# A spectral-mixing and MLP block on one core: folds, gathers and evacuations of the first stage rearranged

**Chip, cores, metric.** One core of a Trainium2 chip (trn2). The metric is the device time of one execution in microseconds; every run here was of the fast state (none was over 1.5% above the fastest of its kernel). "The profile" is one execution recorded on the chip. In its lines PE is TensorE (PEld its weight loads), DVE VectorE, ACT ScalarE, POOL GpSimd, and L241 is line 241 of that run's kernel. TensorE is called *cold* where its 256-column matmuls start 0.21 us apart and *warm* where they start 0.11 us apart; the *granted clock* is the mean TensorE clock that the profile reports, as a share of full speed. A ratio is the mean time of one kernel's runs over the mean of the kernel before's runs of the same rounds on the same chip, so it is not quite the ratio of the medians quoted beside it.

## The reference, cut to what matters

```python
def _A_ref(x, w_r, w_i):                       # x: 1 x 2048 x 512, bf16
    X = rfft2(x.astype(float32), axes=(-2, -1))
    X = X * (w_r + 1j * w_i)                   # 2048 x 257 weights
    return irfft2(X, s=(S, D)).astype(bfloat16)

h  = x + _A_ref(layernorm(x), A_w_r, A_w_i)    # first layer norm, then spectral mixing
h2 = h + mlp_squared_relu(layernorm(h))        # 512 -> 1792 -> 512
```

The transforms are done as matmuls against sine and cosine tables that the kernel computes itself. This case is about the first 26 us: first layer norm, tables, and stage 1 of the forward transform.

## The kernel before: the parts that matter

The 2048 rows lie as 16 groups g of 128. The layer norm's 1/std is not applied to the rows but *folded* into the transform table: `KFr[g] = KF * rs1[g]`. Statistics come from VectorE (13 groups) or ScalarE (groups 3, 7, 11), the root `(var + eps)^-0.5` from GpSimd.

```python
def ln1_rstd(a, b):                            # GpSimd: add, then power -0.5
    nc.gpsimd.tensor_scalar(rs1[:, a:b], mv1[:, a:b, 1], EPS, None, ALU.add)
    nc.gpsimd.tensor_tensor(rs1[:, a:b], rs1[:, a:b], mhalf[:, 0:b - a], ALU.pow)

def ln1_fold(a, b, eng=nc.vector):
    for g in range(a, b):
        eng.tensor_scalar(KFr[:, g, :], KF[:], rs1[:, g:g + 1], None, ALU.mult)

def stage1(g0, n=0, split=False):              # two groups, 8 matmuls; n filler matmuls first
    if split:                                  # two PSUM tiles, evacuated by two engines
        two = [mm_tile("p1a"), mm_tile("p1b")]
        ...
    warm(pts[0], n)
    ...                                        # 8 matmuls xs x KFr into pts
    if split:
        for t, cp in ((0, nc.scalar.copy), (1, nc.vector.tensor_copy)):
            cp(dst[:, 2 * t:2 * t + 2], ...)
        return two[0][:, 512:1024].bitcast(BF16)
    else:
        nc.scalar.copy(dst, ...)               # whole evacuation on ScalarE

def w_reversed(i):                             # indirect DMA issued by GpSimd: the "gather"
    nc.gpsimd.indirect_dma_start(out=WB[i][:, 16:23, :]..., in_=(A_w_r, A_w_i)[i]..., ...)
```

PSUM is the memory that matmuls write to; an *evacuation* copies a tile out of it, and the program keeps four tiles of this size. In the traces each engine runs its list in the order in which it is written: in e2 below, ScalarE stood idle for 2.46 us in front of a sine whose angles were late, with an evacuation that was ready behind it. `angles_g` (GpSimd) and `sin_of(GF)` (ScalarE) make the table that stage 2 needs. The products mA and mB of the spectral loop (VectorE) read the gathered rows from their second round on.

## Time and profile before

| | kernel before |
|---|---|
| time, median of 4 runs | 183.78 us (183.73 to 183.84) |
| span in the profile | 181.9 us |
| TensorE / VectorE / ScalarE / GpSimd busy | 88% / 67% / 56% / 26% |
| first matmul of stage 2 | 22.43 us |
| second mA (VectorE) starts | 29.61 us |
| first matmul of the MLP | 62.37 us |

Busy shares average over stages with different limits. The question for each stage is which wait ends last; for the first 22 us the chain of waits answers it, and the prediction shows those lines.

### The profile page before, as it was taken

The page shows a single profiled execution, that of the slowest core. Times are in us where ns is not written, and L with a number is a line of the kernel's source. Part 1 is how long each engine was busy: PE and PEld are TensorE (multiplying, and loading weights), DVE is VectorE, ACT ScalarE, POOL GpSimd, SP SyncE. Part 2 cuts the span into 40 slices and gives each one's busy share as a digit, 9 for nine tenths or more (in the row PEclk, how much of TensorE's full clock was granted, in tenths as well). Part 3 has the DMA queues.
Part 4 walks back from the last instruction along what each step waited for, and adds up shares of the span by engine and source line. Part 5 has one row for each costly group of instructions (what it writes and reads, how often), then busy time and mean ns, then how long its engine had stood idle before and what let it go on. Part 6 is the DMA issues. An engine that isn't in the chain of part 4 may idle for free.

```text
span 181.9 us, 2667 instructions
## 1 busy us (share of the span) xinstructions
PE 160.0 (88%) x946; PEld 89.0 (49%) x946; DVE 122.2 (67%) x297; ACT 101.8 (56%) x172; POOL 46.5 (26%) x83
## 2 busy tenths in 40 slices
PE   3676896989978787999999999999999989999991
PEld 1244564666534475456643545544544434556440
DVE  7986549999957277646897248697338795359311
ACT  4976879999634278037931367922357921268200
POOL 5889910000000250204402022422022422025000
PEclk9999999999999999999999999999999999999999
DMA  5999990000000000000000000001110000110010
GB/s 159 352 425 405 378 228 23 0 0 4 2 0 0 2 4 0 2 29 29 4 0 29 29 29 4 0 0 50 36 34 0 0 0 29 58 34 0 0 58 29
DMA packets 7773, 11.19 MB, mean 62 GB/s; under 512 B 2256, under 2 KB 6224, under 8 KB 7504
## 3 DMA queue, kind: packets, MB, share of 16 engines
q1 hardware_dynamic: 7600, 10.11, 16.3%
q0 software_dynamic: 160, 0.92, 1.2%
q8 instruction: 7, 0.11, 0.3%
q14 instruction: 6, 0.05, 0.1%
HBM read 8.93 MB, written 2.10 MB: 61 GB/s over the span
## 4 chain that ended last, share of the span: by engine, by line
PE 50%; DVE 29%; ACT 9%; POOL 6%; issue 4%; DVEq 0%; POOLq 0%; ACTq 0%
PE ph L570 22%; PE po L589 20%; DVE act L574 3%; PE p L473 3%; DVE mA L379 3%; DVE mB L379 3%; DVE hs L488 2%; ACT rl L573 2%; ACT Bt L241 2%; PE p L532 2%; DVE st L497 2%; DVE st L205 2%; DVE M L392 2%; DVE Z L384 2%; ACT junk L494 1%
## 5 line engine op out<-in xcount | busy, mean ns | idle before, releaser
L570 PE MATMUL ph<-UT,W 128*128 128x384 bf16 (+2 forms) x280 | 53.2, 336 | 0.7 <-ACT UT L536 0.5
L573 ACT ACTIVATE rl<-ph,b1f 128x384 bf16<-128x384 f32 (+2 forms) x70 | 41.2, 603 | 20.9 <-PE ph L570 19.5
L589 PE MATMUL po<-W,act 128*128 128x512 bf16 x224 | 50.8, 379 | 0.0
L574 DVE TENSOR_TENSOR act<-rl 128x384 bf16<-128x384 bf16 (+2 forms) x70 | 32.5, 477 | 17.2 <-ACT rl L573 16.9
L570 PEld LDWEIGHTS <-W 128*128 128x128 bf16 x280 | 27.4, 98 | 20.8 <-issue 1.4
L589 PEld LDWEIGHTS <-act 128*128 128x128 bf16 x224 | 21.6, 98 | 27.4 <-issue 3.1
L577 POOL TENSOR_TENSOR hb<-hs,b2b 128x512 f32<-128x512 bf16 x16 | 18.4, 1153 | 57.4 <-DVE act L574 55.4
L593 DVE TENSOR_TENSOR ot<-po,hb 128x512 bf16<-128x512 f32 x16 | 11.0, 689 | 18.1 <-PE po L589 18.1
L517 ACT ACTIVATE u<-hs,nm,rs 128x512 bf16<-128x512 bf16 x6 | 4.7, 808 | 25.2 <-DVE nm L514 25.2
L231 PE MATMUL p<-KFr,xs 128*128 128x256 bf16 x28 | 8.6, 334 | 4.7 <-DVE KFr L216 4.6
L488 DVE SCALAR_TENSOR_TENSOR hs<-p,xs 128x512 bf16<-128x512 f32 x16 | 10.8, 678 | 0.1
L473 PE MATMUL p<-GI,T 128*128 128x256 bf16 x64 | 9.4, 272 | 0.4 <-DVE T L415 0.4
L502 POOL TENSOR_TENSOR nm<-mv 128x1 f32<-128x1 f32 x5 | 1.5, 291 | 30.9 <-ACT junk L494 30.9
L246 PE MATMUL idle<-ones 128*128 128x512 bf16 x37 | 9.0, 379 | 0.0
L487 PE MATMUL p<-R,KI 128*128 128x512 bf16 x16 | 6.1, 381 | 3.2 <-DVE R L483 3.2
L233 PE MATMUL p<-KFr,xs 128*128 128x256 bf16 x28 | 8.6, 335 | 0.0
L246 PEld LDWEIGHTS <-ones 128*128 128x128 bf16 x45 | 4.7, 106 | 7.8 <-POOL ones L142 2.9
L205 DVE BATCH_NORM_STATS2 st<-xs 128x6 f32<-128x512 bf16 x13 | 8.3, 673 | 0.0
L360 ACT CAST AB<-p 128x1024 bf16<-128x1024 f32 x7 | 7.1, 1014 | 1.9 <-PE p L358 1.2
L417 ACT CAST T<-p 128x1024 bf16<-128x1024 f32 x7 | 7.2, 1025 | 1.8 <-PE p L410 1.8
L330 PE MATMUL p<-GF,Bt 128*128 128x256 bf16 x64 | 8.1, 273 | 0.0
L473 PEld LDWEIGHTS <-T 128*128 128x128 bf16 x64 | 6.2, 98 | 3.5 <-ACT T L414 0.9
(135 smaller groups left out, 220.5 us busy)
## 6 DMA issues: line engine op xcount, KB each, us to landing
W<-in_B_w_dram SPq DMA_DIRECT2D x2, 1792.0 KB, 19.7
out_dram<-ot SPq DMA_DIRECT2D x16, 128.0 KB, 1.8
xs<-in_A_x_dram SPq DMA_DIRECT2D x3, 512.0 KB, 5.9
WB<-in_A_w_r_dram SPq DMA_DIRECT2D x1, 1028.0 KB, 9.6
WB<-in_A_w_i_dram SPq DMA_DIRECT2D x1, 1028.0 KB, 12.2
xs<-in_A_x_dram SPq DMA_DIRECT2D x2, 256.0 KB, 3.4
b2b<-in_B_b_dram SPq DMA_DIRECT2D x1, 128.0 KB, 8.2
b1b<-in_B_b_dram SPq DMA_DIRECT2D x1, 3.5 KB, 22.8
```

Of the source, the lines that this page charges most:

```text
L205: nc.vector.bn_stats(st[:], xs[:, g, :])
L231: nc.tensor.matmul(o, lhsT=xs[:, g, P * t:P * t + P], rhs=KFr[:, g, 0:P].unsqueeze(1).to_broadcast([P, 2, P]), start=True, stop=False)
L246: nc.tensor.matmul(o, lhsT=ones[:, 0:P], rhs=ones[:], start=True, stop=True)
L379: nc.vector.tensor_tensor(m[:], X[:], w[:, pr:pr + step + 1:step, 1:Df].unsqueeze(2).to_broadcast([P, 2, 2, 256]), ALU.mult)
L473: nc.tensor.matmul(pe[:, 256 - 256 * e:512 - 256 * e], lhsT=T2[:, lt, g].rearrange("p q s -> p (q s)"), rhs=GI[:, lt, :], start=(r == 0), ...
L488: nc.vector.scalar_tensor_tensor(hs[:, g, :], py[:], WSC, xs[:, g, :], ALU.mult, ALU.add)
L570: nc.tensor.matmul(ph[:, 0:n], lhsT=W1[:, d, bass.ts(f, P)], rhs=UT[:, d, 0:n], start=(d == 0), stop=(d == ND - 1))
L573: nc.scalar.activation(rl[:, 0:n], ph[:, 0:n], ACT.Relu, bias=b1f[:, f:f + 1], scale=1.0)
L574: sq = nc.vector.tensor_tensor(act[:, f, 0:n], rl[:, 0:n], rl[:, 0:n], ALU.mult)
L577: add = nc.gpsimd.tensor_tensor(hb[:, g, :], hs[:, g, :], b2b[:], ALU.add)
L589: nc.tensor.matmul(po[:], lhsT=act[:, f, bass.ts(i, P)], rhs=W2[:, f, :], start=(f == 0), stop=(f == NF - 1))
L593: nc.vector.tensor_tensor(ot[:], po[:], hb[:, g, :], ALU.add)
```

## The change

Its intent: take work off GpSimd, which holds up the start. All folds go to VectorE; both gathers are issued behind the last root; ScalarE's three pairs of sums come first; the evacuation of (12, 13) is split between ScalarE and VectorE as that of (14, 15) was; two table copies (KI and EI) move behind the first step of stage 3.

```diff
--- before.py
+++ after.py
@@ -260,50 +260,46 @@
     def table_neg(ks):
         nc.vector.tensor_scalar(EI[:, ks[0]:ks[-1] + 1, 2, :], EI[:, ks[0]:ks[-1] + 1, 0, :], -1.0, None, ALU.mult)
 
-    ln1_sums(3)
-    ln1_sums(7)
+    for g in (3, 7, 11):
+        ln1_sums(g)
     ln1_stats(0, 1)
     ln1_rstd(0, 2)
-    w_reversed(0)
+    angles_g(0)
     ln1_stats(2, 4, 5)
     ln1_fold(0, 2)
     stage1(0, 8)
-    ln1_sums(11)
-    angles_g(0)
     ln1_rstd(2, 6)
-    w_reversed(1)
+    angles_g(1)
     ln1_stats(6, 8, 9)
     ln1_fold(2, 6)
     stage1(2)
     ln1_rstd(6, 10)
-    ln1_fold(8, 10, nc.gpsimd)
-    angles_g(1)
     stage1(4)
     ln1_stats(10, 12)
-    ln1_fold(6, 8)
+    ln1_rstd(10, 12)
+    ln1_fold(6, 10)
+    stage1(6)
+    ln1_stats(13)
+    ln1_fold(10, 12)
+    ln1_rstd(12, 14)
     sin_of(GF[:].rearrange("p t c -> p (t c)"), fiG[:])
-    stage1(6)
-    ln1_rstd(10, 12)
-    ln1_stats(13)
-    ln1_rstd(12, 14)
     stage1(8)
     ln1_stats(14, 15)
-    ln1_fold(10, 12)
     ln1_rstd(14, 16)
+    ln1_fold(12, 14)
+    stage1(10)
     nc.gpsimd.memset(ident[:], 0.0)
     nc.gpsimd.affine_select(out=ident[:], in_=ident[:], compare_op=ALU.not_equal,
                             fill=1.0, base=0, pattern=[[-1, P]], channel_multiplier=1)
-    stage1(10)
-    ln1_fold(12, 14)
-    stage1(12)
+
+    nc.vector.tensor_scalar(GF[:, :, 255:256], GF[:, :, 255:256], 0.5, None, ALU.mult)
     ln1_fold(14, 16)
+    w_reversed(0)
+    w_reversed(1)
     nc.vector.tensor_scalar(EF[:, :, 2, :], EF[:, :, 0, :], -1.0, None, ALU.mult)
-
-    nc.vector.tensor_scalar(GF[:, :, 255:256], GF[:, :, 255:256], 0.5, None, ALU.mult)
+    stage1(12, split=True)
     tr08 = stage1(14, split=True)
     transposed(tr08, (0, 8), True)
-    nc.scalar.copy(KI[:], tr08[:, 4 * P:5 * P])
-    table_i(tr08, (0, 8))
 
     nc.gpsimd.tensor_scalar(cols[:, 4:5], pF[:, 0:1], 256.0, 128.0, ALU.mult, ALU.add)
     nc.gpsimd.tensor_scalar(cols[:, 5:6], pF[:, 0:1], 256.0, 256.0, ALU.mult, ALU.add)
@@ -419,6 +415,8 @@
     stage2(0, split=True)
     stage2(1)
     stage3(0)
+    nc.scalar.copy(KI[:], tr08[:, 4 * P:5 * P])
+    table_i(tr08, (0, 8))
     stage3(1)
     stage2(2)
     tr = mm_tile("ptr", BF16)
```

## The prediction

> **What bounds the kernel now.** I read the page's engine shares first, then the chain of waits in order of time, then the timelines of ScalarE, VectorE and GpSimd over the first 27 us, and last the busy time by stretch. TensorE is busy 88% of the span, but the change touches only the first 26 us, and there the chain of waits runs elsewhere. Its columns are start, length and piece of work:
>
> ```profile
> 9.97 0.54 POOL rs L212
> 10.52 0.70 issue
> 11.22 1.12 POOL WB L145
> 12.38 0.27 POOL rs L211
> 12.72 1.05 POOL rs L212
> 13.88 1.93 POOL KFr L216 x2
> 15.90 0.94 POOL fiG L179 x2
> 16.86 1.06 ACT GF L113
> 17.92 3.68 ACT Bt L241 x4
> 21.60 0.50 ACT Bt L238
> 22.14 0.40 PE p1a L251 x4
> 22.59 1.75 PE p L330 x16
> ```
>
> The path is GpSimd from 9.65 to 16.84 us (second gather L145, inverse roots L211/L212, two folds L216, second half of the angles L179). Then ScalarE takes over until 22.09 us with the sine of those angles (GF) and five stage-1 evacuations that could not pass it in its queue. Then stage 2 (L330) starts. The ScalarE timeline shows the same handover, with the reason for each idle stretch in brackets:
>
> ```profile
> 13.31 1.01 ACT L241 CAST Bt<-p 128x1024 bf16<-128x1024 f32 x1 [0.67 <-PE p L233]
> 15.01 1.01 ACT L241 CAST Bt<-p 128x1024 bf16<-128x1024 f32 x1 [0.69 <-PE p L233]
> 16.86 1.06 ACT L113 ACTIVATE GF<-fiG 128x1024 bf16<-128x1024 int16 x1 [0.84 <-POOL fiG L179]
> 17.83 3.77 ACT L241 CAST Bt<-p 128x1024 bf16<-128x1024 f32 x4
> 21.50 0.59 ACT L238 CAST Bt<-p1a 128x512 bf16<-128x512 f32 x1
> ```
>
> From 26.4 us the bound is VectorE and from 62.4 us TensorE; the busy-time table (PE, PEld, DVE, ACT, POOL) says so:
>
> ```profile
> 26.40:52.10 25.70, 22.23 (x167) 14.79 (x164) 25.49 (x64) 21.66 (x23) 0.27 (x1) 1.00 0.03 6
> 62.40:181.90 119.50, 111.50 (x630) 58.82 (x629) 73.04 (x164) 57.43 (x110) 25.21 (x32) 1.00 0.06 18
> ```
>
> Neither has slack to absorb an earlier start, so whatever the start of stage 2 gains should reach the end nearly whole, and nothing but that start can gain. So the question is one number: when does the first L330 matmul start, which is now 22.43 us?
>
> **What the Trainium skill says.** "SBUF — State Buffer", section "Who interferes with whom": GpSimd shares a port pair with VectorE's two-port modes, and whichever starts second waits. The trace agrees in direction: two VectorE folds beside a GpSimd fold took 0.70 us (at 13.81 us), against 0.48 us alone (at 17.99 us); it is no full block, as a GpSimd fold lasts 0.97 us. "TensorE: Matmul & The Clock Gate", section "Part 1: The HAM clock gate (the “warmup” mystery)": half clock until some 3.4 us of sustained matmuls. The trace agrees: the 256-column matmuls start 0.213 us apart from 11.40 to 14.77 us (3.37 us) and 0.109 us apart from there on. "DMA: Bandwidth & Descriptors", section "Anatomy of one DMA — SWDGE (gpsimd) path", fits 2.0 us plus bytes over 436e3 per us for one DMA. A gather here is 128 x 1799 bf16 values, 460,544 bytes, so 3.1 us; the trace has 7.9 and 7.4 us to landing, beside 400 GB/s of other loads. I use the trace's.
>
> **The change part by part.**
>
> GpSimd loses, before the angles are done, both gathers (1.24 + 1.12 us busy, some 0.4 us of issue around them) and two folds (1.93 us), 4.7 us in all. Its list, followed by hand: first root done at 7.10; angles first half 7.14 to 8.08; roots 2 to 6 wait for ScalarE's sums of g = 3 (8.34) and take 0.23 + 0.09 + 1.06, so 8.39 to 9.77; second half of angles 9.81 to 10.75; roots 6 to 10 to 12.18. So the angles that came at 16.84 are there at 10.75 us, and the sine no longer waits for GpSimd.
>
> VectorE becomes the pacemaker of the folds. Rates from its timeline: three statistics 2.08 us, two 1.42, one 0.82, four folds 0.79, two 0.38. From 8.31: statistics 6, 8, 9 to 10.39; folds 2 to 6 (roots at 9.77, before they waited until 11.06) to 11.18; statistics 10, 12 to 12.60; folds 6 to 10 to 13.39; statistics 13 to 14.21; folds 10, 11 to 14.59; statistics 14, 15 to 16.01; folds 12, 13 to 16.39; the last root comes at 17.22, so folds 14, 15 at about 17.3 to 17.65, if the half-scaling of GF ahead of them is not waiting for the sine (below). The two folds moved here cost VectorE 0.4 us, where GpSimd took 1.93.
>
> TensorE: stage 1 of (2, 3) starts 0.34 us behind its first fold, at 10.73 (was 11.40). Sixteen cold matmuls at 0.213 us last until 14.14; if warmth comes 3.4 us after the start, at 14.1, and at the latest at 14.77 as before, (6, 7) ends at 15.0 to 15.3, (8, 9) at 16.1, (10, 11) at 17.0, (12, 13) at 17.9.
>
> ScalarE: three pairs of sums now come first, 6.78 to 11.17 at 1.46 us each (the third needs its rows by 9.71; the transfers of 512 KB land in 5.9 us at the median, so about 8). An evacuation costs 0.92 us back to back, the sine 0.97, a half evacuation 0.5 to 0.59. Evacuations: (0) 11.17 to 12.08; (2) waits for its matmuls, 12.69 to 13.60; (4) 14.39 to 15.30; (6) 15.4 to 16.3; sine to 17.3; (8) to 18.2; (10) to 19.1; half of (12) to 19.6; half of (14) to about 20.2. It idles perhaps 1.5 us in between, waiting for cold matmuls; this is why I do not book the whole GpSimd gain of 6.1 us.
>
> The end of stage 1: the four PSUM tiles are handed round, and two split stages need four. By the order in the built program (14, 15) takes the tiles of (8, 9) and (10, 11), so its second half starts only when evacuation (10) is done, about 19.15 to 19.3; four matmuls of 0.11 and the tail bring VectorE's half evacuation to 19.9 to 20.6. Splitting (12) moves 0.69 us to VectorE, which is free, and saves ScalarE 0.42. The transposes wait for ScalarE's last half and take 0.29 us, so stage 2 starts at 20.5 to 20.75 by this count. For the shared port I add 0.1: the angles now lie beside the folds at 7.9 and 10.4 us. I take **20.7 us** against 22.43, a gain of **1.7 us**.
>
> Moving the two copies for the inverse tables (KI and EI, 0.16 + 0.48 us) behind the X copy takes them ahead of AB, where ScalarE was idle 0.62 us waiting for L358: by the count it is free 0.07 us before AB is wanted. Value zero.
>
> The gathers now start behind the last root and the identity: 18.0 and 19.2 us. With 7.9 and 7.4 us to land they are there at 25.9 and 26.6. The products that read their rows are the second mA and mB, at 29.61 and 30.20 before, so 27.9 and 28.5 then: 1.9 us to spare. Hidden, but not by much.
>
> Sum: −1.7 us, nothing added elsewhere: 183.8 − 1.7 = **182.1 us**, 0.9%.
>
> **The rivals.** First, **ScalarE without gaps**. It has 11.17 us plus six evacuations, a sine and two halves, 7.6 us, so 18.8 if it never waits; then VectorE's last folds and half evacuation bound stage 2 at 19.7 and the gain is 2.7 us, 181.1. For it: the idle stretches hang on when TensorE gets warm. Against it: the matmuls were cold from 8.26 to 14.77 before, and the gap at 10 us is still there. Second, **the cold clock lasts longer**: if the warm decision falls a window later, up to 0.8 us of the gain goes, 182.9. Third, **the gathers become the wait**: a landing 3 us later than assumed would stop VectorE at the second mA for a microsecond, 183.1, and much later makes it slower than before. For it: they are issued while the W1 and W2 loads still run (387 GB/s from 16.6 to 22.4 us). Against it: those loads die out by about 26 us, and before there were more of them ahead. Fourth, **stage 1 not the end**: if VectorE's spectral loop were held by something else, the gain would vanish; against it stands the table above, 25.49 of 25.70 us busy.
>
> **Range and chances.** The first rival sets the low side, the second and a mild third the high side: 181.3 to 183.1 for 8 in 10. Two per cent is 3.7 us, more than even the gapless count gives: faster 0.04. Slower by 3.7 us would need a gather landing some 7 us late: 0.02. Within 2%: 0.94.
>
> **What would show it right or wrong.** Right: in the changed profile the sine of GF no longer waits for GpSimd; the first L326 matmul (stage 2's new line) starts near 20.7; the second half of stage 1 (14, 15) waits for evacuation (10); from there everything is the old trace moved by the same amount, with stretch lengths of 25.7, 10.3 and 119.5 us kept. Wrong: VectorE idle at the second mA or mB put down to a DMA; the last stage-1 evacuations beginning much before or after 18.2 us; a spectral loop longer than 25.7 us, which would say that ScalarE's AB copies came late behind KI and EI.

## The result, and the profile after

The changed kernel ran in 182.54 us at the median of four runs (182.08 to 182.77), against 183.78: a ratio of 0.9929, interval 0.991 to 0.9949. It lies inside the stated range, 0.44 us above the stated time.

The chain of waits of the changed kernel (start, length, piece):

```profile
1.63 5.12 DMA xs<-in_A_x_dram
6.77 0.69 DVE st L205
...
10.79 0.27 DVE KFr L216
11.10 0.37 PE p L231
...
16.26 1.01 ACT Bt L241
17.28 0.95 ACT GF L113
18.23 1.82 ACT Bt L241 x2
20.05 0.98 ACT Bt L238 x2
21.08 0.40 PE p1a L251 x4
21.53 1.78 PE p L326 x16
```

GpSimd is gone from the start. The path now begins with the landing of the rows at 6.75 us, runs through VectorE's statistics and folds and TensorE's matmuls of stage 1, and ends on ScalarE again. ScalarE's timeline, with what ended each idle stretch in brackets:

```profile
13.00 1.01 ACT L241 CAST Bt<-p 128x1024 bf16<-128x1024 f32 x1 [0.85 <-PE p L233]
14.71 1.01 ACT L241 CAST Bt<-p 128x1024 bf16<-128x1024 f32 x1 [0.69 <-PE p L233]
16.26 1.01 ACT L241 CAST Bt<-p 128x1024 bf16<-128x1024 f32 x1 [0.54 <-PE p L233]
17.17 1.06 ACT L113 ACTIVATE GF<-fiG 128x1024 bf16<-128x1024 int16 x1
18.13 1.92 ACT L241 CAST Bt<-p 128x1024 bf16<-128x1024 f32 x2
```

The sine (GF) waits for nothing any more, but it comes *later* than before, 17.17 instead of 16.86 us, because one more evacuation lies ahead of it and each of the first ones waits for matmuls (0.85, 0.69, 0.54 us). Behind it stand only two whole evacuations and two halves instead of four and one: that is the gain. Stage 2 starts at 21.37 us, 1.06 earlier than before. TensorE's timeline shows why the evacuations wait:

```profile
15.32 0.42 PE L231 MATMUL p<-KFr,xs 128*128 128x256 bf16 x1
15.53 0.42 PE L233 MATMUL p<-KFr,xs 128*128 128x256 bf16 x1
...
15.95 0.27 PE L233 MATMUL p<-KFr,xs 128*128 128x256 bf16 x1
16.06 0.27 PE L231 MATMUL p<-KFr,xs 128*128 128x256 bf16 x1
```

Starts lie 0.21 us apart until about 15.8 us and 0.11 us from there: the cold clock ended a microsecond later than in the kernel before (14.77). It was not cold throughout: the first matmuls of stage 1, from 8.58 us, start 0.11 us apart, and at about 9.1 us, after an idle stretch of 2.40 us and half a microsecond of matmuls, the clock falls back. In the kernel before they were cold from the first one, at 8.26 us. The filler matmuls ahead of them already differ, though no edit touches them (first line before, second line after):

```profile
2.94 3.60 PE L246 MATMUL p<-ones 128*128 128x512 bf16 x8 [2.94 <-POOL ones L142]
2.94 3.25 PE L246 MATMUL p<-ones 128*128 128x512 bf16 x8 [2.94 <-POOL ones L142]
```

From the second round of the spectral loop on, little changes but the time of day. The busy-time table over the same two stages (PE, PEld, DVE, ACT, POOL):

```profile
25.00:51.00 26.00, 22.60 (x169) 15.01 (x168) 25.57 (x64) 22.11 (x24) 20.56 (x1) 1.00 0.10 23
61.20:180.80 119.60, 111.53 (x630) 58.91 (x629) 73.16 (x165) 57.43 (x110) 25.23 (x32) 1.00 0.06 18
```

The second mA starts at 28.45 (was 29.61), the MLP at 61.23 (was 62.37), the span ends at 180.8 (was 181.9): 1.06 us at stage 2 become 1.16, 1.14 and 1.1. (GpSimd's 20.56 us there is a single small cast, 0.27 us in the kernel before; the trace does not show why it is so long, and spans on GpSimd are rough.)

So the bulk of the gain is accounted for. What wanted explaining was that GpSimd's part of the path ended six microseconds earlier and only one came out, and that the runs of the changed kernel spread over 0.69 us where the kernel before spreads over 0.11.

### The profile page after: what moved, and what is told of

Its sections match the earlier page's. It is cut to its first block, busy times and chain, and to the rows that moved or that the text cites. A ratio compares the mean times of both kernels' runs of the same rounds, so it can differ in the third digit from the quotient of the medians.

```text
span 180.8 us, 2668 instructions
## 1 busy us (share of the span) xinstructions
PE 159.7 (88%) x946; PEld 89.3 (49%) x946; DVE 122.8 (68%) x300; ACT 101.1 (56%) x172; POOL 64.8 (36%) x81
## 4 chain that ended last, share of the span: by engine, by line
PE 55%; DVE 21%; ACT 14%; DMA 3%; issue 3%; POOL 2%; SPq 0%; DVEq 0%; POOLq 0%; ACTq 0%
PE ph L568 22%; PE po L587 21%; DVE act L572 3%; DMA xs<-in_A_x_dram 3%; ACT U L333 3%; PE p L471 3%; DVE hs L486 2%; ACT rl L571 2%; PE p L530 2%; ACT AB L356 2%; DVE st L495 2%; DVE st L205 2%; ACT Bt L241 2%; ACT junk L492 2%; POOL rs L503 1%
## 5 line engine op out<-in xcount | busy, mean ns | idle before, releaser
L568 PEld LDWEIGHTS <-W 128*128 128x128 bf16 x280 | 27.4, 98 | 20.7 <-issue 1.4
L446 POOL CAST b1f<-b1b 128x14 f32<-128x14 bf16 x1 | 20.6, 20559 | 5.3 <-DMA b1b<-in_B_b_dram 5.3
L231 PE MATMUL p<-KFr,xs 128*128 128x256 bf16 x24 | 7.8, 348 | 3.5 <-DVE KFr L216 3.5
L502 POOL TENSOR_SCALAR rs<-mv 128x3 f32<-128x3 f32 (+2 forms) x5 | 1.2, 243 | 22.3 <-DVE mv L496 22.2
L233 PE MATMUL p<-KFr,xs 128*128 128x256 bf16 x24 | 7.9, 351 | 0.0
```

The source lines that it names most:

```text
L446: nc.gpsimd.tensor_copy(b1f[:], b1b[:])
L568: nc.tensor.matmul(ph[:, 0:n], lhsT=W1[:, d, bass.ts(f, P)], rhs=UT[:, d, 0:n], start=(d == 0), stop=(d == ND - 1))
```

## The experiments

Theory A: stage 1 is now paced by TensorE, whose clock is cold until a moment that differs from run to run; this costs the missing half microsecond and makes the spread. Rival B: the landing of the rows and the statistics pace it, whatever the clock. Theories C to H concern the single parts. All twelve kernels gave correct results.

### e1_after_warm: keep TensorE busy so that it is warm

```diff
-    stage1(0, 8)
+    stage1(0, 12)
...
-    stage1(2)
+    stage1(2, 6)
```

> The changed kernel with 12 instead of 8 filler matmuls ahead of the first stage-1 pair and 6 fillers ahead of the second, so that TensorE is busy without a long gap from 2.9 us and should be at full clock by 9.8 us. Theory A (the missing half microsecond, and the spread of 0.7 us between the runs, come from the cold clock in stage 1): all matmuls from 11 us on start 0.109 us apart, the evacuations follow without gaps, stage 2 starts near 20 us instead of 21.37, the time is 181.0 to 181.6 us with runs within 0.25 us of each other. Theory B (the late landing of the rows, 6.75 us, and VectorE's statistics set stage 1 whatever the clock): 182.3 us or more, and the same spread as the changed kernel.

Measured: 181.67 us at the median (181.53, 181.59, 181.67, 181.74 and one run of 182.35), ratio 0.9896 (0.9883 to 0.991). The matmuls of stage 1 start 0.11 us apart throughout, and ScalarE's timeline shows the evacuations close up:

```profile
11.15 2.91 ACT L241 CAST Bt<-p 128x1024 bf16<-128x1024 f32 x3
14.30 1.01 ACT L241 CAST Bt<-p 128x1024 bf16<-128x1024 f32 x1 [0.24 <-PE p L233]
15.21 1.06 ACT L113 ACTIVATE GF<-fiG 128x1024 bf16<-128x1024 int16 x1
```

Stage 2 starts at 19.56 us, 1.8 earlier than in the changed kernel. B falls as the cause of the missing half microsecond: in this trace too VectorE waited for the rows (0.21 us, until 6.74). What B names is the next limit, though: with TensorE warm, its matmuls wait for VectorE's folds (0.26 us at 13.23, 0.67 us at 16.68), and the last fold waits 0.79 us for GpSimd's last root. A's time was nearly met, its spread not quite (one run of five lay 0.6 us off; there is no trace of that run). But of the 1.8 us only 0.8 reached the end of the span, and VectorE's timeline shows where the rest went:

```profile
27.02 0.69 DVE L375 TENSOR_TENSOR mA<-X,WB 128x1024 bf16<-128x1024 bf16 x1 [0.15 <-DMA WB<-in_A_w_r_dram,idxR]
28.27 0.69 DVE L375 TENSOR_TENSOR mB<-X,WB 128x1024 bf16<-128x1024 bf16 x1 [0.55 <-DMA WB<-in_A_w_i_dram,idxR]
```

The second mB starts 0.78 us earlier than in the changed kernel (29.05), and that is all that is left: the late gathers have become the wait.

### e2_before_warm and e8_before_kept_warm: the same fillers in the kernel before

e2 puts the two edits of e1 into the kernel before. e8 adds more fillers:

```diff
-    stage1(6)
+    stage1(6, 4)
...
-    stage1(10)
+    stage1(10, 7)
```

> The kernel before with the same fillers. Theory A says that there the sine of GF waits for GpSimd until 16.8 us and the evacuations behind it run back to back, so a faster TensorE gives nothing: 183.8 us, within 0.25 us. Theory B has no opinion on it. If it gains as much as the same fillers in the changed kernel, the clock is worth something by itself and has nothing to do with the change.

> The kernel before with the fillers of e2 and more of them (4 ahead of (6, 7), 7 ahead of (10, 11)) in the gaps in which e2's TensorE fell back to the cold clock at 18.8 us. If e2 was slow from that fallback, and the kernel before is otherwise deaf to the clock: 183.7 us, all runs within 0.3. If the fillers cost by themselves: 184.7 or more as e2.

e2: 184.71 us at the median, ratio 1.0036 (1.0016 to 1.0057). My expectation was wrong for most of its runs. They fall in two groups: four of 184.71 to 184.80, whose mean granted clock is 0.990 or 0.991, and two of 183.71 and 183.76 (clock 1.000 and 0.997). The profiled one is slow, and its TensorE timeline has the reason:

```profile
16.39 0.27 PE L233 MATMUL p<-KFr,xs 128*128 128x256 bf16 x1
18.33 0.28 PE L231 MATMUL p<-KFr,xs 128*128 128x256 bf16 x1 [1.66 <-DVE KFr L216]
...
18.78 0.41 PE L231 MATMUL p<-KFr,xs 128*128 128x256 bf16 x1
18.98 0.42 PE L233 MATMUL p<-KFr,xs 128*128 128x256 bf16 x1
```

Made warm early, TensorE did its work sooner, sat idle for 1.66 us and fell back to the cold clock at 18.78 us, just where the last evacuations wait for it. e8 fills that gap: 183.66 us at the median, ratio 1.0008 (0.9994 to 1.0021), five of six runs between 183.64 and 183.73, the sixth 184.51 with a clock of 0.991. So the fillers cost nothing, the fallback costs one microsecond, and the kernel before gains nothing from a warm TensorE: it waits for GpSimd. Its own runs say the same: eleven runs beside e8, with mean clocks from 0.978 to 1.000, all took 183.65 to 183.76 us.

### a2_after_again: the changed kernel a second time

No edit.

> The changed kernel once more, unaltered, for its spread and a second trace. If the phase of the clock windows sets its time (theory A): its runs spread over 0.5 us or more again, between 182.0 and 182.8, while the kernel before stays within 0.15 us on the same chip; and in the new trace stage 2 starts later by as much as the cold matmuls end later, from 21.37 us at an end of the cold at 15.8.

Measured: 181.95 us at the median (181.60 to 182.39), ratio 0.9905 (0.9891 to 0.9919); the kernel before beside it 183.64 to 183.76. The spread is there again, 0.79 us, though lower than I said at both ends. In its TensorE timeline the cold clock ended earlier:

```profile
14.86 0.36 PE L231 MATMUL p<-KFr,xs 128*128 128x256 bf16 x1
15.06 0.27 PE L233 MATMUL p<-KFr,xs 128*128 128x256 bf16 x1
```

Stage 2 started at 20.91 us and the run took 182.07 us. The first trace had the switch at 15.8, stage 2 at 21.37 and 182.58 us. So an end of the cold clock 0.9 us earlier gave 0.46 at stage 2 and 0.51 at the end; the part of the sentence "by as much as the cold matmuls end later" was too strong, for half-speed matmuls lose only half of the time. (In this trace TensorE was cold from the first matmul of stage 1, 8.56 us, as in the kernel before.) Of the nine runs of this kernel, the three with a mean clock of 0.981 or less took 182.39 to 182.77, the six others 181.60 to 182.49: the two traces and this ordering fit theory A, but a trace was kept of two runs only. The Trainium skill ("TensorE: Matmul & The Clock Gate", section "Part 1: The HAM clock gate (the “warmup” mystery)") says of the window that decides the clock that it is free-running and does not reset with the kernel; the switches at 14.77, 14.9 and 15.8 us in three traces agree with it. Within one trace the switches lie about 3.4 us apart or twice that: about 18.8 and 22.2 us in e2, about 9.1 and 15.8 us in the first trace here.

### e3_folds_only: one part alone

```diff
-    ln1_fold(8, 10, nc.gpsimd)
...
-    ln1_fold(6, 8)
+    ln1_fold(6, 10)
```

> The kernel before with the two GpSimd folds put on VectorE, nothing else. Theory C (GpSimd's list is the path, whatever is taken off it counts until the next wait): the angles are done at 14.9 instead of 16.84 us, the sine starts behind the third evacuation at 15.9, stage 2 starts 0.9 us earlier, 182.9 us. Rival D (the folds alone move nothing since the gathers and the roots still hold GpSimd): 183.5 us or more.

Measured: 182.59 us, ratio 0.994 (0.9926 to 0.9955). Two GpSimd folds moved to VectorE, in the otherwise unaltered kernel before, give 1.08 us at the median: some nine tenths of what the whole change gave in its first measurement (1.24), and about six tenths of the second (183.67 − 181.95 = 1.72). The sine starts at 15.90 instead of 16.86 us, behind the third evacuation as expected, stage 2 at 21.44 instead of 22.43, and this version's runs spread by only 0.33 us.

### e4_gathers_early: the gathers put back

```diff
     ln1_rstd(0, 2)
+    w_reversed(0)
...
     ln1_rstd(2, 6)
+    w_reversed(1)
...
-    w_reversed(0)
-    w_reversed(1)
```

> The changed kernel with the two gathers put back where they stood (behind the first and the second root). Theory C: the roots of 6 to 10 come at 14.8 instead of 12.5 us, VectorE's folds wait for them and everything behind is late: stage 2 near 22 us, 183.3 us. Rival E (GpSimd has slack now that the folds are gone, the gathers' place does not matter): 182.5 us, within 0.3.

Measured: 182.82 us, ratio 0.9953 (0.9938 to 0.9967), four runs within 0.02 us. VectorE's folds wait for GpSimd's roots, as theory C said:

```profile
14.84 0.88 DVE L216 TENSOR_SCALAR KFr<-KF,rs 128x256 bf16<-128x256 bf16 x4 [1.51 <-POOL rs L212]
```

(VectorE's timeline), but against the 182.54 us of the changed kernel the loss was 0.3 us where I expected 0.8: in this trace stage 2 started at 21.51, not near 22. The cold clock ended at 15 us here too, inside a wait for the folds, and cost this version nothing that GpSimd had not cost already; hence, I take it, the runs within 0.02 us. Against the two measurements of the changed kernel (ratios 0.9929 and 0.9905) the late gathers are worth 0.24 to 0.48% of 183.7, so 0.4 to 0.9 us. The first of these is not clear of noise (the intervals overlap), the second is. That it is most when TensorE happens to be warm early is what the account above leads one to expect; no run undoes the gathers with TensorE kept warm.

### e5_warm_ident: e1 with the gathers started sooner

```diff
     ln1_rstd(6, 10)
+    nc.gpsimd.memset(ident[:], 0.0)
...
     ln1_rstd(10, 12)
+    nc.gpsimd.affine_select(out=ident[:], ...)
...
-    nc.gpsimd.memset(ident[:], 0.0)
-    nc.gpsimd.affine_select(out=ident[:], ...)
```

> The kernel of e1 with the identity matrix built in two gaps of GpSimd's list (behind the roots of 6 to 10 and of 10, 11), so that the two gathers start 0.75 us earlier than in e1 (17.5 instead of 18.28 us). Theory F (in e1 the gathers, issued at 18.28 and 19.91 us and 8.6 and 8.3 us in landing, made VectorE wait for 0.15 and 0.55 us at the second mA and mB; they land by when they are issued): both waits gone or under 0.1 us, 180.8 to 181.2 us. Rival G (they land when the W1 and W2 loads leave room, whenever they were issued): the waits stay, 181.5 us or more.

Measured: 181.05 us (180.92 to 181.10 and one run of 181.48), ratio 0.986 (0.9846 to 0.9874). Stage 2 starts at 19.39 us. The wait at the second mA is gone, that at the second mB is 0.31 us. Most of theory F holds, yet the second gather still lands 8.4 us after its issue and ends the wait.

### e6, e7, e9, e10: one part undone in e5

e6 evacuates (12, 13) whole on ScalarE; e7 puts the folds of 8 and 9 back on GpSimd; e9 puts the sums of g = 11 back behind the first evacuation; e10 puts KI and EI back behind the transposes.

```diff
e6: -    stage1(12, split=True)      +    stage1(12)
e7: -    ln1_fold(6, 10)             +    ln1_fold(6, 8)   and ln1_fold(8, 10, nc.gpsimd) behind ln1_rstd(6, 10)
e9: -    for g in (3, 7, 11): ...    +    3 and 7 only; ln1_sums(11) behind stage1(0, 12)
e10:     the two lines KI and table_i(tr08, (0, 8)) directly behind transposed(tr08, (0, 8), True)
```

> e5 with the evacuation of stage 1 (12, 13) whole on ScalarE again. By the count ScalarE's last half starts at 18.9 instead of 18.6 us, while the last matmuls wait for the last root anyhow: 0.1 to 0.3 us slower than e5. Rival: the split matters as the diff suggests, 0.4 us or more.

> e5 with the two folds of 8 and 9 back on GpSimd. Theory C (GpSimd's list is the path again): the roots of 10, 11 end at 15.7 instead of 14.1 us, VectorE's folds of 10, 11 and the statistics behind them are 1.2 us later, and so is everything: 1.0 to 1.3 us slower than e5. Rival (in the clock-safe version GpSimd has slack): under 0.4 us.

> e5 with ScalarE's sums of g = 11 back behind the first evacuation, as before the change. ScalarE does the same work in another order and is caught up before the sixth evacuation: the same as e5 within 0.15 us. If the reordering of the statistics has a value of its own, it is 0.3 us or more slower.

> e5 with the two copies KI and EI back at once behind the transposes. They stand ahead of the first U copy, which then comes 0.2 us later, and not ahead of AB, where the wait is for L354 anyhow: the same as e5 within 0.15 us. If moving them mattered: 0.3 us or more slower.

| | median, us | ratio to the kernel before (95%) | stage 2 starts |
|---|---|---|---|
| e5, all parts | 181.05 | 0.986 (0.9846 to 0.9874) | 19.39 |
| e6, (12) not split | 181.21 | 0.9863 (0.9849 to 0.9877) | 19.72 |
| e7, folds on GpSimd | 182.78 | 0.9949 (0.9935 to 0.9964) | 21.24 |
| e9, sums back | 181.22 | 0.9861 (0.9846 to 0.9876) | 19.38 |
| e10, tables back | 181.33 | 0.988 (0.9865 to 0.9895) | 19.52 |

e7 loses 1.7 us, more than I said: VectorE waits 1.52 us for the roots of 10 and 11, and the second of the sixteen stage-2 matmuls starts only at 21.91. Of the four parts undone here, the folds are the only one that carries weight; the gathers, undone only in e4, are not among the four. The split of (12) starts stage 2 0.33 us earlier, but in e5 the wait for the second gather swallows the difference. The order of the sums shows no effect (0.17 us at the median, just outside my 0.15; the ratios are 0.986 and 0.9861). e10 came out 0.28 us slower at the median, outside my 0.15; its ratio interval overlaps that of e5, and its trace has the first AB copy 4.22 us behind the start of stage 2, where e5 has 4.23, so I can name no mechanism by which it would be slower. A tenth of a per cent stays open there.

### e11_w2_late: clear the way for the gathers

The load of W2 waits for the second mB product instead of standing in the queue from about 5 us on.

```diff
-    nc.sync.dma_start(W2[:], ...)
...
+        if pr == 1:
+            late = nc.sync.dma_start(W2[:], ...)
+            tc.add_manual_dep(late.ins, prod.ins.name, ...Sync...)
```

> e5 with the load of W2 (1.8 MB, first used some 75 us later) issued only after the second mB product. Theory H (the gathers take 8.5 us to land because they share the engines with the W1 and W2 loads): they land in 3 to 6 us, VectorE's wait of 0.31 us at the second mB is gone, 180.6 to 180.9 us. Rival: the landing time is the gather's own, 8 us stay and nothing is gained, or the late load disturbs something: 181.05 us or more.

Measured: 180.91 us (180.78 to 181.06), ratio 0.9852 (0.9837 to 0.9867), the fastest version here, 1.5% under the kernel before; against e5 it is not separated (the intervals overlap). The gathers land in 6.0 and 7.0 us instead of 8.6 and 8.4, and VectorE's timeline has no wait in front of the second mA and mB any more (no bracket):

```profile
26.72 0.68 DVE L374 TENSOR_TENSOR mA<-X,WB 128x1024 bf16<-128x1024 bf16 x1
27.32 0.69 DVE L374 TENSOR_TENSOR mB<-X,WB 128x1024 bf16<-128x1024 bf16 x1
```

The landing shortened less than theory H said: with the DMA engines 54% busy between 17.6 and 26.3 us (98% in e5 between 17.6 and 27.6), 6 to 7 us remain. How much of that is the gather's own is not shown: until 24.0 us the engines were still 72% busy and moved some 1.3 MB (198 GB/s), of which at most 0.92 MB were the gathers. From there to 26.3 us, where the second gather lands, they were 5% busy, so the last 2.3 us are hardly a matter of crowded engines.

## Why the prediction was right, point by point

**The path and what it is worth: right.** The chain named GpSimd, then ScalarE; the sine no longer waits; and what stage 2 gained went through to the end, 1.06 us there and 1.1 at the end of the span. The spectral loop from the second mA to the matmul at its end is 22.5 us long in both traces (29.61 to 52.13, 28.45 to 50.98), so the fourth rival is out.

**GpSimd: right.** The angles were done at 10.97 us (10.03 plus 0.94), against 10.75 by the count.

**VectorE: right but late by a third of a microsecond.** The folds of 2 to 6 began at 10.71, not 10.39. The first 0.23 us of that is a wait for the rows that the profile of before did not have. It is no effect of the change: e2, whose loads and list of VectorE are those of the kernel before, has it too (0.21 us).

The last folds, of 14 and 15, came at 18.34 instead of 17.3, behind the half-scaling of GF, which waited 1.50 us for the sine: the case that the prediction named and did not follow up. It cost nothing that the trace shows, as TensorE waited for a tile, freed by an evacuation, until 19.18.

**TensorE: the term that was mis-sized.** The step "if warmth comes 3.4 us after the start, at 14.1, and at the latest at 14.77 as before" failed. The clock turned at 15.8 in the first trace and at 14.9 in the second. The trace of before had shown one position of the switch, and I read it as the latest. It had also shown that 3.4 us after a start is not enough by itself: its fillers ran for 3.60 us from 2.94 us on, and behind 1.72 us of idle the first stage-1 matmuls were cold. The evacuation of (8) began at 18.13 (17.67 in the second trace) instead of 17.3, and stage 2 at 21.37 (20.91) instead of 20.7. The two traces part the miss: 0.46 us goes with the clock, and the 0.21 us that are left where it turned near the predicted limit go, I take it, with VectorE's delay, for there the evacuation of (2) is already 0.28 us late (12.97 instead of 12.69). I had the late clock as the second rival, at 182.9, and the range covered it. Over its nine runs the kernel lies at 181.60 to 182.77 on both sides of the predicted 182.1: that a set of runs falls near it is in part the luck of the clock's phase.

**The end of stage 1: right in kind.** In TensorE's timeline the second half of (14, 15) waits for the evacuation of (10):

```profile
20.10 0.27 PE L231 MATMUL p1b<-KFr,xs 128*128 128x256 bf16 x1 [0.32 <-ACT Bt L241]
```

**KI and EI, value zero: right within what can be told.** AB starts 4.08 us after stage 2, was 4.07. One line moved: the 0.50 us of idle before the first mA is gone, and 0.21 us of waiting for AB stand at the next step, so 0.1 us is the net of it. e3, which leaves KI and EI where they were, has the same pattern, so it is not due to their move. By its letter one sign of being wrong came up: from the first mA the loop takes 26.0 us (24.98 to 50.93) and not 25.7, as its first product starts 1.46 us earlier than before and its second round only 1.16. It does not mean what the prediction said it would, since e3 has it too (25.04 to 50.98). Why the first mA waited in the kernel before is not settled.

**The gathers: hidden, as said, but not by the stated 1.9 us.** They landed at 25.4 and 28.3 us (18.32 plus 7.1, 19.86 plus 8.4) where 28.45 and 29.05 were wanted: 3.0 and 0.8 us to spare. The second was issued 0.66 us and landed 1.7 us later than I had it. That 0.8 us is why the third rival stayed away in the changed kernel and arrived in e1, as soon as something else became faster.

**The first rival, ScalarE without gaps, 181.1 us: nearly right as a bound.** With TensorE kept warm, stage 2 starts at 19.39 to 19.56 us, 0.1 to 0.3 us below that count (19.7), and e5 takes 181.05. ScalarE idled 2.08 us between evacuations in the first trace, where 1.5 were forecast.

## What to carry to other kernels

Taking work off an engine that ends a chain is worth the distance to the next wait behind it, not the work: 4.7 us of GpSimd's list gave 1.2 to 1.7 us, because TensorE's cold clock and then ScalarE's queue stood right behind. Where matmuls sit on the path early in a kernel, try a handful of fillers in the gaps: here they took the clock out of play (e1), but in the kernel before, where one gap of 1.66 us stayed open, the fallback came later and at a worse place (e2). A transfer that is "hidden" needs its spare time written down (0.8 us here), since the next improvement spends it.

## What the Trainium skill lacked or had wrong

- "TensorE: Matmul & The Clock Gate", Part 1: it advises not to fit a cold count since the ramp is under 1% of a typical span. That holds here (0.9 us of cold clock moved the time by 0.51 of 182 us), but the spread that goes with it, 0.69 and 0.79 us in the two sets of runs, is more than half of the 1.24 us that the change was first measured to gain. Its table lets the cold clock come back after at least one idle window of about 3.4 us. Here less sufficed: the clock fell back about half a microsecond after an idle stretch of 1.66 us in e2 and of 2.40 us in the first trace of the changed kernel. Which stretch suffices no run settles: 1.61 us at nearly the same time did not in the kernel before.
- "DMA: Bandwidth & Descriptors", "Anatomy of one DMA — SWDGE (gpsimd) path": the fit gives 3.1 us, as an estimate, for one gather of 460,544 bytes; the runs show 7.1 to 8.7 us beside the weight loads and 6.0 and 7.0 us with the engines 54% busy. I found no figure for indirect gathers.
- "SBUF — State Buffer", "Who interferes with whom": it says that, where VectorE is in a two-port mode, the second of two instructions fully blocks; two VectorE folds beside a GpSimd fold of 0.97 us took 0.70 us, less than a full block. That the folds are in such a mode is not shown. (The 0.48 us that the prediction calls "alone" lay beside GpSimd's small root instructions; with GpSimd idle, at 8.26 us in the changed kernel, two folds took 0.47.)
- No page that I read says that the mean granted clock of a profile leaves out a cold start: the kernel before is given 1.000 while its 256-column matmuls start 0.21 us apart until 14.77 us. Only a fall from warm to cold shows up (0.978 in the first trace of the changed kernel). The profile of e8 has 1.000 too, and was warm from 8.60 us on: a clock of 1.000 does not tell the two apart.
